# Column factors of the folded weights: on-chip transfers from ScalarE's queue in place of contraction-of-one products

## The chip, the core and the metric

The kernel runs on one core of one Trainium2 chip. The metric is the device time of the whole program in microseconds (us). The core has five engines that matter here: TensorE (PE in the profile) multiplies, with its weight loads listed apart as PEld; VectorE (DVE) and ScalarE (ACT) do elementwise work and empty the PSUM banks; GpSimd (POOL) does elementwise work in on-chip memory; SyncE (SP) issues nearly all transfers. ScalarE can issue transfers too. Whoever issues them, they are carried out by 16 DMA engines.

## The reference, cut to what matters

```python
X = np.fft.fft(np.fft.fft(x, axis=1), axis=2).real     # x: (8, 3008, 256) float32
h = X.reshape(24064, 256) @ w_in                       # w_in: (256, 2048)
g = h * (1.0 / (1.0 + np.exp(-1.702 * h)))             # quick gelu
out = g @ w_out                                        # w_out: (2048, 256)
```

A Fourier mixing over positions and channels is followed by a two-layer block with a quick gelu. Both weight matrices reach the kernel as 64-bit values, viewed as pairs of 32-bit words; the kernel makes float32 values of them on the chip.

## The kernel before, in words

**What is computed where.** The transform along the 256 channels is never done on the data. It is folded into the first weights: `fold_w(n)` (line 457) multiplies the tables `cd` with 512 columns of `w_in`, and `wcs[0]` and `wcs[1]` (each 128 x 2048) receive the cosine and the sine half. The transform along the 3008 positions is done on the data in two steps (`mix_first` or `mix1`, then `stage2`) and gives `pq`, blocks of 512 positions. Row 0 of the sine half is special: there the data row carries the alternating-sign component, which belongs neither to cosine nor to sine. `nyquist` (line 357) spreads that data row over all 128 partitions (`nb`), and its weights, row 0 of `wcs[1]`, are needed as a column, one value for each hidden unit on its own partition. These are the column factors: `af1` (128 x 16, column f for hidden units 128 f to 128 f + 127) and `af2`, twice that.

**How the columns are made.** `first_row(n)` (line 467) makes four columns. For each, a product with a contraction of one turns a 1 x 128 piece of row 0 into a 128 x 1 column of a PSUM bank (`psf`), with the constant `twos` as the other operand. Two ScalarE instructions then take the four columns out of the bank: a copy into `af2` (line 472) and a copy scaled by 0.5 into `af1` (line 473). There are four such groups, n = 0 to 3.

**The main loop.** `steps` numbers the work: 8 batches, 3 blocks of positions, 2 halves of a block and 8 pairs of hidden blocks (NP = 8). The first 8 steps (t = 0 to 7) take the weights while they are still being made. Step t runs `hidden(t)` (two banks `pa` and `pb`, 16 products; ScalarE copies `pa` to `v`), `rows(t)` on VectorE (which needs `v`, `nb` and two columns of `af2`, and ends with `reversed_sum`, line 539), `activate(t)` on ScalarE one step later, and `product(t - 3)`, which multiplies by `w_out`. From step 8 on, `middle(t)` writes `nb` times `af1` into a bank (line 566) before TensorE adds to it, and the second product is done with fewer multiplications (lines 596 to 671).

**Weights arriving.** `load_in(n)` and `load_out(n)` (lines 370 and 375) load a quarter of a weight matrix, 1 MB each. `clamp` (POOL), `squares`, `low_up` and `low_down` (ACT) and `high` (DVE) turn the 64-bit values into float32, and `finish_in` or `finish_out` (POOL) adds the parts. `load_in(2)` and `load_in(3)` feed `fold_w(2)` and `fold_w(3)`, which are placed in steps 3 and 5.

**What sets the order.** Each engine takes its instructions in program order, and the order is written out by hand: prologue, then the loop with the tables `extra`, `early` and `rows_at`. `early` says in which step `fold_w` runs, `rows_at` in which step `first_row` runs (before: n = 0 in the prologue, n = 1, 2, 3 in steps 1, 4 and 6). PSUM banks without a fixed tag are taken in turn from the list `spare`, so an allocation that is dropped moves all later ones. In step 5 the list is cut to four banks, and `hidden(5)` takes two others by name.

**Transfers.** SyncE issues in this order around the change: spill of the first batch's mixed rows to DRAM (`spill_first`, line 305), `fill` (line 328) which brings them back transposed in two parts, `load_out(0)`, `load_in(2)`, eight more spill pieces, `load_out(1)`, the second `fill`, `load_in(3)`, `load_out(2)`, `load_out(3)`, `load_matrices`, and then the input of the second batch (`turn` and `load_x`, lines 185 to 196). All transfers, from either queue, take eight completion semaphores in turn. The issue of a transfer first waits until the transfer before it on the same semaphore, eight places earlier, has landed, and a queue does not pass a waiting instruction.

Of the kernel before, what the change touches and what calls it, by code (L numbers as in the profile page):

```python
# [27 lines left out]
F32 = mybir.dt.float32  # L28
U32 = mybir.dt.uint32
ALU = mybir.AluOpType  # L30
ACTF = mybir.ActivationFunctionType
# [15 lines left out]
def view(ap, offset, *dims):  # L47
    return bass.AP(ap.tensor, ap.offset + offset, [list(d) for d in dims])


def free(ap, offset, *dims):
    return bass.AP(ap.tensor, ap.offset + offset, [list(ap.ap[0])] + [list(d) for d in dims])
# [59 lines left out]
def kernel(ctx: ExitStack, tc, x, w_in, w_out, tab1, tab2, out):  # L112
    nc = tc.nc
# [7 lines left out]
    const = ctx.enter_context(tc.tile_pool(name="const", bufs=1, space=SB))  # L121
# [17 lines left out]
    wcs = [const.tile([128, DF], F32, tag=f"wcs{i}", name=f"wcs{i}") for i in range(2)]  # L139
# [2 lines left out]
    wo, wt = wot[:, 0], wot[:, 1]  # L142
    af1, af2 = (const.tile([128, NF], F32, tag=f"af{i}", name=f"af{i}") for i in (1, 2))
    ones = const.tile([1, 128], F32, tag="ones", name="ones")
    twos = const.tile([1, 1], F32, tag="twos", name="twos")

    psu = ExitStack()
    o_banks = [psp.tile([128, 512], F32, tag=f"o{i}", name=f"o{i}") for i in range(2)]
# [6 lines left out]
    def ring(tag):  # L155
        at, size, count = rings[tag]
        i = turns[tag] = turns.get(tag, -1) + 1
        return big[:, at + i % count * size:at + (i % count + 1) * size]
# [7 lines left out]
    def bank(name, tag=None):  # L166
        if tag is None:
            tag = spare.pop(0)
            spare.append(tag)
        if tag in ("o0", "o1"):  # L170
            return o_banks[int(tag[1])]
        return (rest if tag[0] == "o" else psp).tile([128, 512], F32, tag=tag, name=name)
# [140 lines left out]
    def warm(n):  # L313

        ps = bank("warm")
        for _ in range(n):
            nc.tensor.matmul(ps[:], lhsT=wcs[0][:, 0:128], rhs=wcs[0][:, 0:512], start=True, stop=True)
# [65 lines left out]
    def prepare(key):  # L383


        pre[key] = ring("s"), ring("m"), ring("r").bitcast(U32)
# [70 lines left out]
    def fold_w(n):  # L457
        ps = [bank("psw") for _ in range(2)]
        for i in range(2):
            for cs in range(2):  # L460
                nc.tensor.matmul(ps[cs][:], lhsT=cd[:, i, cs, :], rhs=wst[n][:, i, :], start=(i == 0), stop=(i == 1))
        for cs in range(2):

            nc.scalar.copy(wcs[cs][:, n * 512:(n + 1) * 512].rearrange("p (f c) -> p f c", f=4),
                           free(ps[cs][:], 0, [1, 4], [4, 128]))

    def first_row(n):

        ps = bank("psf")
        for f in range(4 * n, 4 * n + 4):  # L470
            nc.tensor.matmul(ps[:, f:f + 1], lhsT=wcs[1][0:1, f * 128:f * 128 + 128], rhs=twos[:], start=True, stop=True)
        nc.scalar.copy(af2[:, 4 * n:4 * n + 4], ps[:, 4 * n:4 * n + 4])
        nc.scalar.activation(af1[:, 4 * n:4 * n + 4], ps[:, 4 * n:4 * n + 4], ACTF.Copy, scale=0.5)


    NP = NF // 2
# [8 lines left out]
    def width(t):  # L485

        return 226 if steps[t][1:3] == (0, 1) else 256

    def two(ap, n):
        return free(ap, 0, [256, 2], [1, n])  # L490
# [42 lines left out]
    def reversed_sum(out, by, x, y, n, op):  # L533

        full, rest = divmod(n, RUN)
        for at, blocks, m in ((0, full, RUN), (full * RUN, 1, rest)):
            if m:
                ins = [free(z[:], at, [256, 2], [RUN, blocks], [1, m]) for z in (x, y)]
                nc.vector.tensor_tensor(free(out, at + m - 1, [by, 2], [RUN, blocks], [-1, m]), *ins, op=op)  # L539

    def rows(t):
        b, blk, hh, p = steps[t]
        n = width(t)
        nb, ks = nbt[b, blk], slice(hh * 256, hh * 256 + n)
        v, pa, pb = vb.pop(t)
        h = ht[t] = ring("h").rearrange("p (a f n) -> p a f n", a=2, f=2)
        dif = sp.tile([128, 512], F32, tag="v", name="dif")
        nc.vector.tensor_tensor(two(h[:], n), two(v[:], n), two(pb[:], n), op=ALU.add)
        for i in range(2):
            f = 2 * p + i  # L550
            nc.vector.scalar_tensor_tensor(dif[:, i * 256:i * 256 + n], nb[:, ks], af2[:, f:f + 1],
                                           pb[:, i * 256:i * 256 + n], op0=ALU.mult, op1=ALU.subtract)
        reversed_sum(h[:, 1, 0], 256, pa, dif, n, ALU.add)

    def activate(t):
        g = free(ht[t][:], 0, [256, 4], [1, width(t)])
        nc.scalar.activation(g, g, ACTF.Gelu_apprx_sigmoid)
# [11 lines left out]
    def begin(t, cs=0):  # L569

        n = width(t)
        for i in range(2):
            halves(xb[t][:, i * 256:i * 256 + n], *operands(t, cs, i), start=False, stop=(cs == 1))
# [13 lines left out]
    def activate_back(t):  # L587
        nc.scalar.activation(back(t), back(t), ACTF.Gelu_apprx_sigmoid)  # L588
# [239 lines left out]
    for e in odds:  # L828
# [1 line left out]
    nc.vector.memset(flat[:, 6144:6176], 0.0)  # L830
    nc.vector.memset(free(pair[:, 0, 0], 0, [2 * NJ * NM, 2], [16 * 2 * NM, 2], [1, 2 * NM]), 0.0)
    nc.vector.memset(ones[:], 1.0)
    nc.vector.memset(twos[:], 2.0)
    ends = n0 + 4 - 28 * NM
    nc.sync.dma_start(out=free(w0, 0, [28 * NM, 2], [1, ends]),
                      in_=view(tab1, 0, [tab1.shape[1], 128], [28 * NM, 2], [1, ends]))
# [47 lines left out]
    warm(1)  # L884
    fold_w(0)
    warm(1)
    first_row(0)
    prepare(out0)
    finish_in(1)
    clamp(out0)  # L890
# [19 lines left out]
    n = len(steps)  # L910
# [4 lines left out]
            at(t - 1, bounds, key)  # L915
        at(t + 1, finish, key)
    early[3], early[5] = 2, 3
    rows_at = {1: 1, 4: 2, 6: 3}
    for t, c in ((0, 2), (1, 3)):
        at(t, load_out, c, nc.sync)  # L920
    at(3, load_matrices)
# [29 lines left out]
    for t in range(n + LAG):  # L951
        if t < NP:
            if t == NP - 3:
                spare[:] = [tag for tag in spare if tag[0] == "o"] + ["b2"]
            hidden(t)
            if t == NP - 1:
                middle(NP)
                begin(NP)
                nc.gpsimd.memset(wcs[1][0:1, :], 0.0)
            if t == 0:  # L960
                low_up(in2)
                nyquist(0, 0)
                low_down(in2)
            if t in rows_at:
                first_row(rows_at[t])
            if t >= LAG:
                product(t - LAG, 0, None)
            if t in early:
                fold_w(early[t])
            if t:  # L970
                activate(t - 1)
            rows(t)
            if t == NP - 1:
                doubled(NP)
                middle(NP + 1)
        else:
            after, special = (any(fn in (mix1, stage2) for fn, _ in extra.get(k, ())) for k in (t - 1, t))
            if t < n:
                begin(t, 1)
            if t == NP:  # L980
                activate(t - 1)
            if t < n:
                forward(t)
            if after and t + 1 < n:
                middle(t + 1)
            opening = (t - LAG) % NP == 0 and t >= NP + LAG
            one, other = (t - LAG, (1, 2, 4, 7)), (t - LAG - 1, (5, 6, 3))
            if opening:
                small_products(*other)
            cut = 0 if opening and not after else 3 if after else 2  # L990
            product(t - LAG, 0, cut)
            if after:
                small_products(one[0], one[1][:1])
                small_products(other[0], () if opening else other[1][:1])
            if t + 1 < n:
                begin(t + 1)
            if not opening:
                small_products(other[0], other[1][after:])
            product(t - LAG, cut, 6 if t - LAG == last else None)
            small_products(one[0], one[1][after:])  # L1000
            swap(t - LAG - 2)
            if t < n:
                backward(t)
            if t + 1 < n:
                doubled(t + 1)
            if t < n:
                activate_back(t)
                sums(t, nc.gpsimd)
            if t + 2 < n and not special:
                middle(t + 2)  # L1010
            combine_small(t - LAG - 1)
            if t - LAG == last:
                product(last, 6, None)
            sums(t - 1, nc.vector)
            deeper(t - 2, 0)
            deeper(t - 3, 1)
        if t == NP:
            psu.close()
            low = ctx.enter_context(tc.tile_pool(name="low", bufs=1, space=PS))
            pot["low"] = low.tile([128, 3 * 512], F32, tag="low", name="low")  # L1020
        if t >= LAG:
            combine(t - LAG)
            combine_last(t - LAG - 2)
            turn_last(t - LAG - 3, 0)
            turn_last(t - LAG - 4, 1)
        if t >= NP:
            spare[:] = [f"b{t % 2}"] * special + ["b2"]
        for fn, args in extra.get(t, ()):
            fn(*args)
# [28 lines left out]
```

## Time and profile before

The time before is 1876.94 us, the median of 3 runs (1874.98 to 1878.47). The profiled execution has a span of 1875.6 us.

| engine | busy us | share of the span | instructions |
|---|---|---|---|
| PE | 1853.0 | 99% | 23600 |
| PEld | 1414.9 | 75% | 23600 |
| DVE | 1532.0 | 82% | 2245 |
| ACT | 1148.9 | 61% | 2248 |
| POOL | 962.4 | 51% | 1058 |

The share is an average over the whole span. The columns are made in its first 80 us, where other things can set the pace. The table by stage shows the difference; each number is busy time in the stretch, and DMA is the mean busy share of the 16 DMA engines.

| stretch, us | PE | DVE | ACT | POOL | DMA share | what runs |
|---|---|---|---|---|---|---|
| 26 to 40 | 12.28 | 9.09 | 9.96 | 8.09 | 0.81 | folds 0 and 1, columns 0 |
| 40 to 49 | 9.00 | 7.33 | 7.42 | 3.64 | 0.91 | steps 0 to 2, columns 1 |
| 49 to 57 | 7.31 | 7.48 | 6.45 | 4.41 | 1.02 | step 3, fold 2 |
| 57 to 64 | 6.75 | 6.79 | 5.87 | 3.69 | 0.94 | step 4, columns 2 |
| 64 to 73 | 9.00 | 5.87 | 1.81 | 4.68 | 0.76 | step 5, fold 3 |
| 73 to 80 | 7.00 | 1.70 | 6.19 | 1.06 | 1.04 | step 6, columns 3 |
| 400 to 1000 | 598.89 | 498.51 | 373.24 | 302.59 | 0.36 | main loop |

In the main loop TensorE is busy nearly all the time, so a delay in the first 80 us that moves the start of the loop moves the end. The line of a group in the profile names the engine, the tile written and the tile read; the text after `[idle before <-` says what ended the idle time ahead of it. The wait of a transfer's issue is listed under SPq.

### The profile page before, as it was taken

The numbers are of one execution on the slowest core, as the hardware profiler recorded it, in microseconds if no ns is written. First come the engines' busy times: TensorE is split into PE (matmuls) and PEld (weight loads), VectorE is DVE, ScalarE is ACT, GpSimd is POOL, SyncE is SP. The second block draws the span as 40 slices with busy tenths as digits, with TensorE's granted clock in tenths as the row PEclk, the third lists the DMA queues.
The fourth block names the chain that finished last, engine by engine and source line by source line (L and its number), as shares of the span: only waits on it lengthen the run. The fifth ranks groups of instructions, "written<-read, shape, count | busy, mean of one in ns | idle before, by whom it ended". The sixth has DMA issues, their size and how long they took to land.

```text
span 1875.6 us, 55597 instructions
## 1 busy us (share of the span) xinstructions
PE 1853.0 (99%) x23600; PEld 1414.9 (75%) x23600; DVE 1532.0 (82%) x2245; ACT 1148.9 (61%) x2248; POOL 962.4 (51%) x1058
## 2 busy tenths in 40 slices
PE   8999999999999999999999999999999999999998
PEld 5567778777777777777777777777778777778776
DVE  7788878888789877988788877898788888878874
ACT  6655655666666666666565666656666656656663
POOL 4577335744467443673347733485435754444442
PEclk9999999999999999999999999999999999999999
DMA  8732351336221362305513165042631231212211
GB/s 275 180 51 17 80 88 20 51 51 115 27 17 47 52 123 19 52 17 94 80 16 52 23 115 56 13 63 44 111 26 24 19 51 47 28 16 18 20 22 23
DMA packets 145415, 105.21 MB, mean 56 GB/s; under 512 B 104914, under 2 KB 127986, under 8 KB 143984
## 3 DMA queue, kind: packets, MB, share of 16 engines
q1 hardware_dynamic: 143952, 101.14, 32.7%
q8 instruction: 186, 3.05, 0.7%
q10 hardware_dynamic: 1216, 0.52, 0.1%
q14 instruction: 61, 0.50, 0.1%
HBM read 58.38 MB, written 48.01 MB: 57 GB/s over the span
## 4 chain that ended last, share of the span: by engine, by line
PE 89%; DVE 5%; ACT 3%; DMA 2%; issue 1%; POOL 0%; SPq 0%; DVEq 0%; ACTq 0%; POOLq 0%
PE x L495 33%; PE o L495 25%; PE low L659 23%; PE o L659 4%; DMA big<-in_moe_w_in_dram 2%; DVE big L625 2%; PE ps L246 1%; PE ps L348 1%; DVE big L762 1%; DVE big L539 1%; ACT x L566 1%; ACT xt L249 0%; DVE big L671 0%; ACT big L581 0%; PE po L495 0%
## 5 line engine op out<-in xcount | busy, mean ns | idle before, releaser
L596 POOL TENSOR_TENSOR big<-big 128x256 f32<-128x256 f32 (+1 forms) x376 | 348.7, 927 | 848.9 <-ACT big L588 731.3
L495 PE MATMUL x<-pq,wcs 128*64 128x256 f32 (+1 forms) x6016 | 778.0, 378 | 5.7 <-ACT x L566 3.1
L625 DVE TENSOR_TENSOR big<-big 128x512 f32<-128x512 f32 (+1 forms) x736 | 640.0, 884 | 30.9 <-PE low L659 14.5
L495 PE MATMUL o<-big,wo 128*64 128x256 f32 (+1 forms) x4800 | 628.4, 376 | 0.4 <-DVE big L603 0.3
L495 PEld LDWEIGHTS x<-pq,wcs 128*64 128x64 f32 x6016 | 416.4, 137 | 194.1 <-issue 14.6
L495 PEld LDWEIGHTS o<-big,wo 128*64 128x64 f32 x4800 | 346.2, 137 | 147.7 <-DVE big L603 1.2
L578 ACT ACTIVATE g<-x 128x512 f32<-128x512 f32 (+1 forms) x376 | 221.7, 590 | 376.1 <-PE x L495 375.0
L539 DVE TENSOR_TENSOR big<-g,x 128x512 f32<-128x512 f32 (+2 forms) x440 | 254.2, 589 | 204.3 <-ACT big L581 203.6
L659 PE MATMUL low<-big 128*64 128x128 f32 (+1 forms) x5888 | 385.0, 270 | 1.9 <-issue 1.9
L659 PEld LDWEIGHTS low<-big 128*64 128x64 f32 x5888 | 340.2, 137 | 30.1 <-issue 2.1
L566 ACT ACTIVATE x<-nb,af 128x256 f32<-128x256 f32 (+1 forms) x752 | 352.7, 469 | 12.2
L597 POOL TENSOR_TENSOR big<-big 128x256 f32<-128x256 f32 (+1 forms) x376 | 358.9, 954 | 0.0
L581 ACT ACTIVATE big<-x 128x512 f32<-128x512 f32 (+1 forms) x376 | 220.4, 586 | 202.5 <-PE x L495 180.3
L588 ACT ACTIVATE big<-big 128x512 f32<-128x512 f32 (+1 forms) x376 | 231.8, 616 | 44.4 <-DVE big L539 43.1
L659 PE MATMUL low<-big,wo 128*64 128x128 f32 (+1 forms) x2944 | 223.3, 271 | 0.1
L659 PEld LDWEIGHTS low<-big,wo 128*64 128x64 f32 x2944 | 175.0, 137 | 3.6 <-DVE big L625 0.4
L604 DVE TENSOR_TENSOR big<-big 128x512 f32<-128x512 f32 (+1 forms) x188 | 149.9, 798 | 6.5
L603 DVE TENSOR_TENSOR big<-big 128x512 f32<-128x512 f32 (+1 forms) x188 | 137.1, 729 | 4.6 <-POOL big L596 4.6
L659 PEld LDWEIGHTS o<-big,wo 128*64 128x64 f32 x1472 | 94.4, 138 | 24.9 <-issue 0.3
L659 PE MATMUL o<-big,wo 128*64 128x128 f32 (+1 forms) x1472 | 112.4, 272 | 0.1
L762 DVE TENSOR_TENSOR big<-big,low 128x512 f32<-128x512 f32 (+3 forms) x184 | 109.1, 610 | 3.5
L218 POOL TENSOR_TENSOR xt<-xt 111x510 f32<-111x510 f32 x56 | 78.2, 1397 | 4.4
(103 smaller groups left out, 973.2 us busy)
## 6 DMA issues: line engine op xcount, KB each, us to landing
out_dram<-os SPq DMA_DIRECT2D x284, 64.0 KB
Td<-xt SPq DMA_DIRECT2D x14, 768.0 KB
t<-Td SPq DMA_DIRECT2D x7, 1536.0 KB
xt<-in_x_dram SPq DMA_DIRECT2D x14, 512.0 KB
xt<-Xr SPq DMA_DIRECT2D x14, 512.0 KB
nb<-pq SPq DMA_DIRECT2D x23, 256.0 KB
out_dram<-os SPq DMA_DIRECT2D x96, 56.0 KB
Xr<-in_x_dram SPq DMA_DIRECT2D x7, 752.0 KB
```

Source lines behind the costliest of these rows:

```text
L495: nc.tensor.matmul(out[c0:c0 + 64], lhsT=lhs[:, c0:c0 + 64], rhs=rhs, skip_group_check=True, **how)
L539: nc.vector.tensor_tensor(free(out, at + m - 1, [by, 2], [RUN, blocks], [-1, m]), *ins, op=op)
L566: nc.scalar.activation(x[:, i * 256:i * 256 + n], nbt[b, blk][:, hh * 256:hh * 256 + n], ACTF.Copy, scale=af1[:, f:f + 1])
L578: nc.scalar.activation(two(g[:], n), two(xb[t][:], n), ACTF.Copy, scale=2.0)
L581: nc.scalar.activation(front(t), two(xb[t][:], width(t)), ACTF.Gelu_apprx_sigmoid)
L588: nc.scalar.activation(back(t), back(t), ACTF.Gelu_apprx_sigmoid)
L596: eng.tensor_tensor(right(t, S1, n), left(t, A21, n), right(t, A22, n), op=ALU.add)
L597: eng.tensor_tensor(left(t, S3, n), left(t, A11, n), left(t, A21, n), op=ALU.subtract)
L603: eng.tensor_tensor(s2, s1, a11, op=ALU.subtract)
L604: eng.tensor_tensor(s4, a12, s2, op=ALU.subtract)
L625: nc.vector.tensor_tensor(out, i0, i1, op=how)
L659: nc.tensor.matmul(o, lhsT=lhs, rhs=rhs, start=first_in, stop=(p == NP - 2), skip_group_check=True)
```

## The change

The columns are no longer made by products. After `fold_w(n)` has copied 512 columns into `wcs[1]`, ScalarE's queue issues four transfers, each from 128 values in a row of partition 0 to one column of `af1` on 128 partitions, 4 bytes a piece. `first_row(n)` becomes one ScalarE instruction that doubles four columns of `af1` into `af2`. Its place moves: in the loop it now stands after `activate(t - 1)` and ahead of `rows(t)`, and n = 0 moves from the prologue to step 0. The 16 products, four PSUM banks, the constant `twos` and four ScalarE copies go. The purpose is to free TensorE and the banks from work that only moves values.

```diff
+        for f in range(4 * n, 4 * n + 4):
+            nc.scalar.dma_start(out=af1[:, f:f + 1], in_=free(wcs[1][0:1, f * 128:(f + 1) * 128], 0, [1, 128], [1, 1]))
 
     def first_row(n):
 
-        ps = bank("psf")
-        for f in range(4 * n, 4 * n + 4):
-            nc.tensor.matmul(ps[:, f:f + 1], lhsT=wcs[1][0:1, f * 128:f * 128 + 128], rhs=twos[:], start=True, stop=True)
-        nc.scalar.copy(af2[:, 4 * n:4 * n + 4], ps[:, 4 * n:4 * n + 4])
-        nc.scalar.activation(af1[:, 4 * n:4 * n + 4], ps[:, 4 * n:4 * n + 4], ACTF.Copy, scale=0.5)
+        nc.scalar.activation(af2[:, 4 * n:4 * n + 4], af1[:, 4 * n:4 * n + 4], ACTF.Copy, scale=2.0)
...
     fold_w(0)
     warm(1)
-    first_row(0)
     prepare(out0)
...
-    rows_at = {1: 1, 4: 2, 6: 3}
+    rows_at = {0: 0, 1: 1, 4: 2, 6: 3}
...
-            if t in rows_at:
-                first_row(rows_at[t])
             if t >= LAG:
                 product(t - LAG, 0, None)
             if t in early:
                 fold_w(early[t])
             if t:
                 activate(t - 1)
+            if t in rows_at:
+                first_row(rows_at[t])
             rows(t)
```

The added loop stands at the end of `fold_w`. The dropped lines for `twos` (its allocation and its memset) are left out of the diff.

## The prediction

> **What bounds the kernel now.** The page's list of engines puts TensorE at 99% of the span, so I read first the chain that ended last, to see whether this holds in the first 80 us, where the edit is. It does not. The chain in order of time (start us, length us, what) from 28 us on:
>
> ```profile
> 28.95 8.80 DMA big<-in_moe_w_in_dram
> ...
> 37.77 3.75 DMA Td<-e
> ...
> 41.59 0.38 SPq L328
> ...
> 42.06 10.86 DMA big<-in_moe_w_in_dram
> ...
> 52.95 1.16 ACT big L391
> ...
> 57.25 1.08 PE pa L495 x8
> 58.34 0.86 PE pb L495 x8
> 59.20 0.98 PE psf L471 x8
> ```
>
> The reader is to see that until 52.95 the end is set by transfers in SyncE's queue, one handing over to the next: `load_in(2)` lands, the last spill piece may go, when it has landed the second `fill` may go, behind it `load_in(3)`, and that landing starts the ScalarE work that leads to `fold_w(2)`'s weights and `hidden(4)` at 57.25. From there the chain is TensorE nearly without a gap. Next, SyncE's waits between 25 and 60 us (who waited for what: us in total, times, longest):
>
> ```profile
> SPq L305 <- DMA big<-in_moe_w_in_dram: 3.0, 1, 3.0
> ```
>
> The spill piece reads `e`, which was ready at 25.5; it waits for a weight load only because both use one completion semaphore. So the semaphore a transfer gets can put it on the path. Last, the timeline of ScalarE and of SyncE's issues around 40 us (start, length, instruction, idle before):
>
> ```profile
> 25.51 0.36 ACTq L305 DMA_DIRECT2D Td<-e  x1
> 38.19 0.36 SPq L378 DMA_DIRECT2D big<-in_moe_w_out_dram  x1
> 39.80 0.58 ACT L464 COPY wcs<-psw 128x512 f32<-128x512 f32 x1 [0.27 <-PE psw L461]
> 59.13 1.05 PE L471 MATMUL psf<-twos,wcs 1*128 1x1 f32 x8
> ```
>
> The weights row of `fold_w(1)` is complete at 39.80 + 0.58 = 40.38, later than the last spill (37.77) and `load_out(1)` (38.19) are issued.
>
> **What the Trainium skill says.** "Perfetto Trace Analysis", section "DMA Instruction — HWDGE (DVE, Sync)": the profiled window of a transfer is the issue alone; the move and the completion write come after it. The trace agrees: 0.36 us is shown for the spill at 25.51, but the fill that needs it starts at 27.92. "DMA: Bandwidth & Descriptors", section "Queues, rings and completion order": SP and ACT each own a row of rings on the same 16 DMA engines, so ScalarE's transfers do not pass for free; here the engines are 0.91 busy from 40 to 49 us. "TensorE: Matmul & The Clock Gate", section "What's actually happening": an idle window of about 3.4 us halves the clock. The trace shows a case: after TensorE's 2.20 us idle before 109.32 the granted clock is 0.50 to 0.56 from 109.5 to 113.
>
> **The change part by part.**
>
> *Products removed.* Four groups of about 1.05 us of TensorE (4.2 us). The first (32.06) and second (44.50) lie while the chain is in transfers: nothing. Those at 59.20 and 74.94 are on the chain, 0.98 us each: at most -2.0 us.
>
> *Hand-over of semaphores.* I read the queues of the built changed kernel. The four transfers after `fold_w(1)` come, in the turn of eight, one turn ahead of the last spill (which now waits for the first of them), `load_out(1)` (for the second), the second `fill` (the third) and `load_out(2)` (the fourth). SyncE does not pass a waiting issue. So the first transfer's landing replaces that of `load_in(2)` as what releases the last spill.
> - Issue: from 40.4, when the copy ends. One issue costs 0.36 (row above) to 0.55 us (the median of the 128-partition `nb` transfer); I take 0.42, so they start at 40.4, 40.8, 41.2 and 41.7.
> - Landing, counted from the issue: no row shows a 4-byte transfer. The spill above took 27.92 - 25.51 = 2.4 us with 64 KB to DRAM. Packets on SyncE's queue cost 32.7% of 16 x 1875.6 us over 143,952, or 68 ns each; 128 pieces over 16 engines are 8 x 68 ns = 0.55 us. The skill's DMA page puts a fixed 2.0 us (a fit for GpSimd's path, section "Anatomy of one DMA — SWDGE (gpsimd) path"). I take 2.0 + 0.6 = 2.6; ends 1.9 and 4.
> - Last spill: 40.4 + 2.6 = 43.0 instead of 37.77. `load_out(1)`: the later of 40.8 + 2.6 and 43.0 + 0.45, so 43.5 instead of 38.19, +5.3. `fill`: the spill's 2.4 us on, 45.4 instead of 41.59, +3.8. `load_in(3)`: 45.9 instead of 42.06, +3.8.
> - Landing of `load_in(3)`: by its issue +3.8; by the data ahead of it, which starts with `load_out(1)` after the engines have run empty, +5.3 less about 0.3 for the dip that lay between `load_out(1)` and `fill` (the engines are 0.76 busy from 42 to 44 us). The data are ahead in the ring, so I take +5.0: 57.9 instead of 52.92. Ends 3.8 and 7 from the landing's ends.
>
> ScalarE is free by then: its wait for `load_out(1)` ends near 50, and `low_up`, `low_down`, the copy of `v` and one gelu follow by 55. `hidden(4)` starts at 62.3.
>
> *Order on ScalarE, step 4.* The four issues after `fold_w(2)` (1.7 us) stand ahead of two gelus and `v`, and `af2` now stands behind the gelu of step 3. Counted from `hidden(4)`, `af2` is there at 5.0 to 6.1 us, VectorE needs it at 5.73 as before, so `rows(4)` ends at about 7.3 to 7.5. Before, TensorE went on with `hidden(5)` at 64.03 - 57.25 = 6.78 without waiting for `rows(4)`; with the `psf` banks gone the turn of banks gives it the bank that `rows(4)` still reads. So the 0.98 us saved is lost in a wait: +0.7 net.
>
> *Order on ScalarE, steps 5 to 7.* After `fold_w(3)` ScalarE has no gap from 73.10 to 79.3, then 1.11 us idle. Four issues add 1.7; that idle falls away; the other 0.98 us of TensorE no longer counts, because `middle(8)` on ScalarE releases it: 1.7 - 1.1 - 0.1 = +0.5 net.
>
> *Clock.* TensorE's gap ahead of `hidden(4)` grows from 0.70 to some 3.7 us, and two gaps of 1.6 and 2 us appear. A halved window of 3.4 us costs up to 1.7 us; the first is mostly under the wait of step 4; a quarter of one: +0.4, an estimate.
>
> *At nothing.* The changed `first_row(0)` delays `rows(0)` by about 2 us, and with it the fold of `load_in(2)`: `psw` would run 55 to 58.7, under the wait to 62.3. The loads of the second batch are issued up to 16 us later (one waits for the transfers after `fold_w(3)`) but are first read on GpSimd at 110.40, some 12 us after they would land. Later semaphore turns are the same, as 16 transfers are two full turns.
>
> Sum: 5.0 + 0.7 + 0.5 + 0.4 = +6.6; 1876.94 + 6.6 = 1883.5 us.
>
> **The rivals.**
> - *Only the products count.* The columns land early enough to hold nobody. For it: they are 512 bytes each. Against it: their issue cannot come before 40.38, and the spill they hold left at 37.77. Then -2.0: 1874.9, no slower.
> - *Only ScalarE's issue time counts*: `load_in(3)` has slack or catches up, because the engines serve a shorter queue. For it: the engines dip to 0.76 from 42 to 44. Against: the chain goes through that landing. Then +0.7 + 0.5: 1878.1.
> - *The turned columns are slow.* For it: the `nb` transfer, which also reads one partition, moved 79 packets between 96 and 102 us, 76 ns each one after another with all engines shown busy; 128 pieces in such a row would be 9.7 us. Against: those packets have 2 KB, so the port's rate, 27 GB/s, explains them. At 25 ns a piece a landing takes 5 us and four in a row queue up: about 8 us for the landing, +10.5 on the load and some 2.5 behind it; 1876.94 + 13 = 1890.
>
> **How the numbers follow.** Forecast 0.72, only products 0.08, only issue time 0.08, slow columns 0.12. The forecast's own ends are 3.8 + 0.7 + 0.3 = +4.8 (1881.7) and 7 + 1.1 + 0.9 + 1.7 = +10.7 (1887.6). The range reaches down to the second rival and up to the third: 1878 to 1890; about 0.16 is left outside. Faster by over 0.2% means below 1873.2, which no case gives by itself: 0.05. Within 0.2% (to 1880.7) lie two rivals less that share, and a little of the forecast: 0.15. Slower: 0.80.
>
> **What would show it.** Right: the last spill issued near 43 and waiting for a transfer into `af`; `load_in(3)` landing near 58; TensorE idle 3 to 4 us ahead of `hidden(4)`; a wait of TensorE on VectorE's `rows(4)` ahead of `hidden(5)`; issues of 0.36 to 0.55 us. Wrong: `load_in(3)` landing within 1 us of 52.9, or an `af2` instruction waiting many us for its columns.

## The result, and the profile after

The changed kernel takes 1891.65 us (median of six runs, 1884.83 to 1896.26) against 1877.56 us (1874.98 to 1878.47) on the same chip: ratio 1.0078, 95% interval 1.0057 to 1.0099. It is slower, as predicted, but by 14.1 us where 6.6 were predicted, and it lies 1.65 us above the top of the range.

The chain that ended last in the kernel after, in order of time (start us, length us, what); its lines are one to three lower than those of before, so L466 is the transfer and L470 the doubling in `first_row`:

```profile
41.38 0.50 ACTq L466
...
43.90 0.59 ACT v L507
...
45.93 1.06 ACT big L405
...
46.99 0.10 ACT af L470
...
47.12 0.88 DVE dif L548 x2
...
50.82 2.12 DVE big L422
...
55.16 2.37 POOL wst L436
...
57.57 5.41 PE psw L460 x8
...
65.44 2.06 DMA af<-wcs
...
81.89 3.46 DMA af<-wcs
...
92.50 1.77 PE x L492 x8
```

The reader is to see that SyncE's row of transfers, which carried the chain of before up to 52.95, is gone from it. In its place stand the four issues on ScalarE, then `v(0)` behind them, then the doubling `af2` behind `low_down`, then VectorE's `rows` and `high`, GpSimd's sum and `psw` of `fold_w(2)`. The two pieces `DMA af<-wcs` are landings of columns, but ScalarE itself issues or computes all through both, and e11 and e16 below show that nobody loses by them. TensorE, in the timeline of its instructions (start, length, instruction, idle before and what ended it), waits in four places in this stretch; the line at 62.90, `hidden(4)`, has no wait:

```profile
48.86 1.08 PE L492 MATMUL pb<-pq,wcs 128*64 128x256 f32 x8 [2.46 <-DVE big L536]
...
57.57 5.40 PE L460 MATMUL psw<-wst,small 128*128 128x512 f32 x8 [2.44 <-POOL wst L436]
62.90 1.08 PE L492 MATMUL pa<-pq,wcs 128*64 128x256 f32 x8
...
70.51 1.08 PE L492 MATMUL pa<-pq,wcs 128*64 128x256 f32 x8 [1.90 <-DVE t L334]
...
92.50 1.77 PE L492 MATMUL x<-pq,wcs 128*64 128x226 f32 x8 [4.21 <-ACT x L563]
```

Three of these four are followed by products that take longer than their kind: `psw` 5.40 us in place of 3.70, for one. The clock record has three stretches of 3.4 us at half clock there, from 58.1, 71.8 and 92.3 us; before had its first at 109.6. The length of these stretches agrees with the window of about 3.4 us of which the Trainium skill speaks in "TensorE: Matmul & The Clock Gate", "What's actually happening". The waits ahead of them do not: the skill has the clock halved after an idle window of that length, and here 2.44 and 1.90 us of idle were enough, while 2.46 us ahead of 48.86, 2.54 us in e1 and 2.58 us in e13 were followed by full speed. So the length of a wait alone does not decide it in these traces.

ScalarE's timeline and the summary of its sixteen issues (shortest, median and longest in ns, first and last start) show the price of an issue, and the waits of SyncE (who for what: us in total, times, longest) show the hand-over of semaphores that the prediction had built on:

```profile
41.38 2.48 ACTq L466 DMA_DIRECT2D af<-wcs  x4
43.90 0.59 ACT L507 COPY v<-pa 128x512 f32<-128x512 f32 x1 [2.55 <-PE psn L364]
...
56.79 1.15 ACT L390 ACTIVATE big<-big 128x1024 f32<-128x1024 f32 x1 [1.39 <-DMA big<-in_moe_w_in_dram]
...
62.14 0.59 ACT L463 COPY wcs<-psw 128x512 f32<-128x512 f32 x1 [1.61 <-PE psw L460]
...
81.89 3.45 ACTq L466 DMA_DIRECT2D af<-wcs  x4
```

```profile
L466 ACTq DMA_DIRECT2D af<-wcs x16: 477/618/1632, 32.7 to 84.7; - x16
```

```profile
SPq L304 <- DMA af<-wcs: 7.6, 3, 5.0
...
SPq L377 <- DMA af<-wcs: 1.7, 1, 1.7
```

A group of four issues takes 2.51, 2.48, 2.44 and 3.45 us of ScalarE. Fifteen of the issues take 0.48 to 0.63 us; one in the last group takes 1.63. The other six kernels below that issue the sixteen transfers from ScalarE also have one of 1.1 to 1.6 us in the last group; what it waits for, the profile does not show. Three spill pieces wait 7.6 us together for transfers into `af`, one of them 5.0, and `load_out(1)` 1.7 more; the first reader of `load_in(3)` starts at 56.79 in place of 52.95. But the copy of `wcs` at 62.14 does not wait for the work behind that load, it waits for `psw`, and TensorE goes from `psw` to `hidden(4)` at 62.90 without idle time. So the late load holds nobody there. Where the distance to the kernel before builds up, from the starts of these products in the two traces:

| first product of | before, us | after, us | later by |
|---|---|---|---|
| `hidden(0)` | 39.70 | 40.66 | 1.0 |
| `psw`, `fold_w(2)` | 52.85 | 57.57 | 4.7 |
| `hidden(4)` | 57.25 | 62.90 | 5.7 |
| `hidden(5)` | 64.03 | 70.51 | 6.5 |
| `psw`, `fold_w(3)` | 69.36 | 77.53 | 8.2 |
| step 8 (`x`) | 81.91 | 92.50 | 10.6 |
| step 9 (`x`) | 86.18 | 98.31 | 12.1 |

The rest comes in the main loop, and there the distance does not stay the same. Counted at the starts of the `nb` transfers it is 12.1 us at 94 us of the kernel before, 10.2 at 329, 15.8 at 480, 13.0 at 1085 and 14.2 at 1756. One of the jumps is in TensorE's timeline of the changed kernel: it stands idle for 3.52 us ahead of 422.42, with no wait that the profile shows. So the loop itself moves the distance between these two traces by 2 to 4 us.

### The profile page after: what moved, and what is told of

It reads as the page before. It is cut to its first block, busy times and chain, and to the rows that moved or that the text cites. A ratio compares the mean times of both kernels' runs of the same rounds, so it can differ in the third digit from the quotient of the medians.

```text
span 1889.7 us, 55550 instructions
## 1 busy us (share of the span) xinstructions
PE 1853.0 (98%) x23568; PEld 1420.7 (75%) x23568; DVE 1532.3 (81%) x2244; ACT 1149.8 (61%) x2244; POOL 962.5 (51%) x1058
## 4 chain that ended last, share of the span: by engine, by line
PE 89%; DVE 5%; ACT 3%; DMA 2%; issue 1%; POOL 0%; ACTq 0%; SPq 0%; DVEq 0%; POOLq 0%
PE x L492 33%; PE o L492 25%; PE low L656 23%; PE o L656 4%; PE ps L347 1%; PE ps L245 1%; DVE big L622 1%; PE psw L460 1%; ACT x L563 1%; DVE big L759 1%; DVE big L536 1%; DMA big<-in_moe_w_in_dram 1%; ACT xt L248 1%; DMA wo<-in_tab_dram 0%; ACT big L578 0%
```

## The experiments

Times are medians; "over before" is the difference to the median of the kernel before on the same chip (1876.2 to 1877.0 us), and the interval is that of the ratio. A and B are the two theories at the start: A, ScalarE spends its own time in order on the issues and what stands behind them comes late; B, the prediction's, the semaphores handed to SyncE make its loads late. C, D and L came up on the way.

**What the columns are worth if they cost nothing (e1).** The four `nc.scalar.dma_start` of `fold_w` are taken out, and the columns with them: `af1` and `af2` hold constants.

```
+    nc.vector.memset(af1[:], 1.0)
+    nc.vector.memset(af2[:], 2.0)
-        for f in range(4 * n, 4 * n + 4):
-            nc.scalar.dma_start(out=af1[:, f:f + 1], in_=...)
     def first_row(n):
-        nc.scalar.activation(af2[...], af1[...], ACTF.Copy, scale=2.0)
+        pass
```

> The changed kernel with the sixteen transfers taken out; af1 and af2 are filled once with 1 and 2, and first_row does nothing. Left out of the computation: the column factors themselves. This is the benefit of the change alone, without its price. Theory A (the time of ScalarE in order is the price) and theory B (the hand-over of completion semaphores to SyncE is the price) both say 1874 to 1878 us, load_in(3) landing near 53, psw of fold_w(2) starting near 53 and middle(8) near 82. Above 1884 us both fall: then taking the products away, and the turn of the PSUM banks that goes with it, would itself be what costs.

Measured: 1880.83 us, 3.8 over before, ratio 1.0019 (1.0012 to 1.0026). It falls between the two limits that were set, but nobody had expected a loss: with no transfer left, taking the products away alone makes the kernel slower.

**ScalarE's time without transfers (e2).** As e1, `first_row` kept, and in the place of the issues:

```
+        for _ in range(4):
+            nc.scalar.copy(wst[n][:, 0, :], small[:, 0:512])
```

> As the kernel with free columns, but in the place of the four issues ScalarE makes four copies of 128x512 to a dead tile, of about 0.6 us each; first_row stays where the change put it. Left out: the column factors. No transfer, so no semaphore is handed over and nothing waits for a landing. Theory A (ScalarE's time): 1884 to 1891 us, load_in(3) lands near 53 yet psw(2) starts at 56 to 58 and TensorE stands idle ahead of it. Theory B (hand-over): 1874 to 1879 us.

Measured: 1884.66 us, 7.7 over before, 1.0045 (1.0033 to 1.0058), and `psw` at 57.6, 15.8 us after `hidden(0)` (13.1 in e1 and before). As A said, at the lower end, though half of the loss was already in e1.

**The transfers on SyncE (e3).** `nc.scalar.dma_start` becomes `nc.sync.dma_start`.

> The changed kernel with the same sixteen transfers issued by SyncE's queue. ScalarE has none of the 10 us of issues; SyncE waits for wcs in its own order, so its loads are at least as late as after the change. Theory A (ScalarE's time): 1876 to 1882 us, though load_in(3) lands at 56 or later. Theory B (late loads of SyncE): 1886 us or more, with psw(2) at 57 or later.

Measured: 1896.37 us, 19.4 over before, 1.0109 (1.0095 to 1.0122). A's number is missed by far, and B's (1886 or more, `psw` at 57 or later) is met: `psw` starts at 60.64. But the cause is not B's. ScalarE's timeline of this kernel:

```profile
100.28 0.20 ACT L470 ACTIVATE af<-af 128x4 f32<-128x4 f32 x1 [10.79 <-DMA af<-wcs]
```

On SyncE's queue the last columns stand behind loads, and ScalarE stands 10.8 us ahead of the last doubling, as it stood 3.7 us ahead of the first. The run says nothing on A against B.

**The half-clock stretches (e4).** Ten unused products in the gaps, so that TensorE has something to run:

```
+        if n == 2:
+            warm(3, ps[0])          # ahead of psw of fold_w(2)
...
+            if t == NP - 3:
+                warm(2, bank("warm", "b2"))
             hidden(t)
+            if t == NP - 1:
+                warm(5, bank("warm", "b1"))
```

> The changed kernel with ten products added that are used by nothing, in TensorE's three gaps: three ahead of psw of fold_w(2), two ahead of hidden(5), five ahead of middle(8)'s begin. The waits stay as they are. If the stretches at half the TensorE clock (58 to 62, 72 to 75 and 92 to 96 us in the changed kernel) come from the gaps and each costs 1.5 to 1.8 us: 1885 to 1888 us and at least two of the three stretches gone. If the stretches come by themselves or cost nothing: 1890 to 1894 us.

Measured: 1890.10 us, 13.1 over before, 1.0077 (1.0064 to 1.0089). All three stretches are gone (granted clock 0.996 to 1.000 over the runs, 0.993 to 0.997 in the changed kernel), and the time hardly moves. In the profiles this kernel is 2.8 us quicker from `hidden(0)` to step 9, and gives back 1.7 us of that by the first of the `low` products (at 125 us). So the stretches go when the gaps are filled, and removing them in this way is not worth their length.

**The addresses (e5, e6, e7).** All profiles of the changed kernel and of e1 to e4 started later than before (`hidden(0)` at 40.7 to 43.7 us, not 39.7), and taking `twos` away had moved `xt`, `big` and what lies behind them 32 bytes down. That was theory C. e5 and e7 put a tile back into the place; e6 takes it from the kernel before (shortened):

```
e5, e7: +    pad = const.tile([1, 1], F32, tag="pad", name="pad")
e6:     -    twos = const.tile([1, 1], F32, tag="twos", name="twos")
        -    ... rhs=twos[:] ...   copy to af2, scale=0.5 to af1
        +    ... rhs=ones[:, 0:1] ...   scale=2.0 to af2, copy to af1
```

> The changed kernel with a tile of the size of twos kept in its place and used by nothing. Taking twos away moved xt, big and all tiles behind it 32 bytes down in SBUF; this moves them back. Theory C (the addresses cost): in the profiles of the changed kernel and of e1 to e4 the load of w_in was issued at 9.3 to 11.3 us against 8.6 before and hidden(0) began at 40.7 to 43.7 us against 39.7; with the pad hidden(0) is back near 39.7 and the time falls by 1 to 4 us, to 1887.5 to 1890.5. Rival (the late start comes from run to run): 1890 to 1893 us, hidden(0) anywhere from 39.7 to 43.

> The kernel before without twos: its products of contraction one take a column of ones in its stead, af2 takes the factor of 2 on ScalarE and af1 none. As many instructions on each engine as before, the same values, but the tiles behind twos lie 32 bytes lower, as in the changed kernel. Theory C: 1878.5 to 1881 us and hidden(0) later than 40.5. Rival: 1876 to 1878 us.

> e1 (columns for nothing; their making is left out) with the pad. Theory C: 1875 to 1878 us, hidden(0) near 39.7, so that the benefit of the products taken away is 0 to 2 us and all of e1's 3.6 us over before were addresses. Rival: as e1, 1880 to 1882 us, and the products taken away bring a loss by some other way, the banks' turn or the place of first_row.

Measured: e5 1889.12 us, 12.8 over before, 1.0063 (1.0050 to 1.0075); e6 1875.79, 0.6 under, 0.9995 (0.9987 to 1.0003); e7 1881.83, 5.5 over, 1.0027 (1.0017 to 1.0038). C falls: e6 has the lower addresses and no loss, and e7 has the old ones, an early start (`hidden(0)` at 39.5) and e1's loss. e5's number lies in the range that C had given, but its `hidden(0)` is at 41.1, not back near 39.7, and its 12.8 us are not told apart from the changed kernel's 14.1. The start differs from run to run, and a delay there need not reach the end: e6's profile has `hidden(0)` 2.5 us later than before and its end 0.4 us later. It is the slowest of thirteen runs of e6, so it does not show that a late start costs nothing.

**The turn of the banks (e9, e10).** The products took a PSUM bank from the list `spare` four times. Without them every later tile gets another bank. e9 is e1, e10 the changed kernel, each with one step of the list in those four places:

```
     warm(1)
+    spare.append(spare.pop(0))
     prepare(out0)
...
+            if t in (1, 4, 6):
+                spare.append(spare.pop(0))
             if t >= LAG:
```

> e1 (columns for nothing; their making is left out), with the list of spare PSUM banks moved on by one at the four places where the kernel before took a bank for the products. No instruction more than e1, every later tile in the bank that it had before. Theory D (the banks' turn is what makes e1 and e7 slower than before by 3.6 to 5.5 us): 1874 to 1878 us, and hidden(5) no longer waits for the copy of psr. Rival E (the same loss by something else that went with the products): 1880 to 1882 us.

> The changed kernel with the banks' turn of before restored in the same way, nothing else. Theory D with losses that add up: 1885 to 1888 us. If the turn's loss lies beside that of ScalarE's issues, or theory D is wrong: 1889 to 1893 us.

Measured: e9 1875.14 us, 1.0 under before, 0.9995 (0.9987 to 1.0004); e10 1886.16, 10.0 over, 1.0050 (1.0038 to 1.0063). D holds: one step in a list of names, and e1's loss is gone. TensorE's timeline of e7, where the turn is not restored:

```profile
64.79 1.65 PE L491 MATMUL pa<-pq,wcs 128*64 128x256 f32 x8 [2.56 <-DVE t L335]
66.17 1.98 PE L491 MATMUL pb<-pq,wcs 128*64 128x256 f32 x8
```

and of e9, where it is:

```profile
62.52 1.08 PE L490 MATMUL pa<-pq,wcs 128*64 128x256 f32 x8
```

`hidden(5)` is given the banks b0 and b1 by name. In the turn of before, `psw` of `fold_w(2)` had used them last, and ScalarE had long copied that out. In the new turn it is `hidden(4)`, whose sums VectorE still reads in `rows(4)`: 2.56 us of waiting, and half clock after it. (The trace names the copy into `t`, which VectorE runs right behind `rows(4)`.)

**One transfer for a group (e8, e12).** The row is copied on one partition in the order in which the columns want it, so that 128 pieces of 16 bytes make the whole group, and `first_row` is put ahead of the gelu, for the first group ahead of `fold_w(1)` (that line is not shown); e8 has the pad, e12 the banks' turn:

```
-        for f in range(4 * n, 4 * n + 4):
-            nc.scalar.dma_start(out=af1[:, f:f + 1], ...)
+        nc.scalar.copy(wst[n][0:1, 0, :], ps[1][0:1, :])
+        nc.scalar.dma_start(out=af1[:, 4 * n:4 * n + 4], in_=free(wst[n][0:1, 0, :], 0, [4, 128], [1, 4]))
...
+            if t in rows_at:
+                first_row(rows_at[t])
             if t:
                 activate(t - 1)
-            if t in rows_at:
-                first_row(rows_at[t])
```

> The changed kernel with the pad, one transfer for a group instead of four (a copy of the sum's row on one partition, then 128 pieces of 16 bytes), and first_row put ahead of the gelu, for the first group ahead of fold_w(1). ScalarE's price for a group falls from 2.5 us to about 1.2 and the doubling stands behind nothing. Theory A (ScalarE's time and order is the price): 1878 to 1883 us, middle(8) by 86 and psw(2) by 55. Theory B (hand-over of semaphores, which stays): above 1886 us.

> The changed kernel with one transfer of 16-byte pieces for a group, first_row ahead of the gelu and for the first group ahead of fold_w(1), as in e8 but without its pad, and the banks' turn of before restored. The whole computation. Theory D: 1878 to 1882 us against 1884.0 of e8, so near before but not below it, as the products taken away are worth 2 us at most. Rival E: 1883 to 1886 us.

Measured: e8 1884.01 us, 7.7 over before, 1.0036 (1.0024 to 1.0048); e12 1882.02, 5.8 over, 1.0030 (1.0020 to 1.0041). e8 falls between the two theories, e12 at the upper edge of D's range. ScalarE in e12 ahead of step 7:

```profile
74.21 0.57 ACT L465 COPY wst<-psw 1x512 f32<-1x512 f32 x1
74.81 0.48 ACTq L466 DMA_DIRECT2D af<-wst  x1
...
82.01 0.20 ACT L470 ACTIVATE af<-af 128x4 f32<-128x4 f32 x1 [1.93 <-DMA af<-wst]
```

A group costs 1.1 us in place of 2.5, and here the landing, some 7 us after the issue, holds ScalarE.

**Landings, late loads and ScalarE's time apart (e11, e13 to e16).** e11 and e16 send the transfers into an unread tile (`out=af1` becomes `out=dump`, `af1` filled with ones), e16 with the banks' turn of before. e13 is the kernel before with four transfers of SyncE held back; e14 is e2 with the turn of before; e15 is e14 with the transfers held back as in e13 (shortened: the lines that keep each load's place in its ring are left out):

```
e13, e15:
-    load_out(1, nc.sync); fill(0, 4, NG)       # ahead of the loop
-    load_in(3, nc.sync)
             hidden(t)
+            if t == 1:
+                nc.scalar.copy(raw["out", 1][:, 0:1, 0].bitcast(F32), ones1[:])
+                load_out(1, nc.sync)
+                fill(0, 4, NG)
+                load_in(3, nc.sync)
+                load_out(2, nc.sync)
```

> The changed kernel with all sixteen transfers issued by ScalarE as there, but into a tile that nobody reads; af1 is filled with ones and doubled in the same place (left out: the column factors). ScalarE's issues and the semaphores handed to SyncE stay, nobody computes on what lands. Theory L (the rest between e2, 1884.7 us, and the changed kernel, 1889 to 1892 us, is the wait of af2 and of middle(8) for the landing, 1.9 to 3.5 us after the issue): 1883 to 1886.5 us. Theory B (that rest is the hand-over of semaphores, late loads): 1888 to 1892 us, with load_in(3) landing near 57.

> The kernel before with load_out(1), fill(0, 4), load_in(3) and load_out(2) sent by SyncE only after ScalarE's copy v(1), by one small copy of 128x1 on ScalarE ahead of them that writes where load_out(1) lands: load_out(1) goes out at 45, load_in(3) at 46 in place of 42.1, and lands at 56 to 57, as in the changed kernel. The whole computation. The prediction's step (late load_in(3) holds psw(2) and with it hidden(4)): 1880 to 1883 us and psw(2) at 57. Theory A (it waits beside other work, VectorE's chain of rows and high sets psw(2)): 1875.5 to 1878.5 us with psw(2) at 52.5 to 54.

> e9 (columns for nothing, left out of the computation; the banks' turn of before) with e2's four copies of 128x512 on ScalarE for each group. ScalarE's time alone against 1875.1 us of e9. Theory A: 1879 to 1883 us. If ScalarE's time costs only together with the other banks' turn: 1875 to 1877.5 us.

> e14 with the four loads of e13 sent late in the same way. If ScalarE's time and late loads together make what is left of the change (e10, 1886.2 us): 1884.5 to 1888 us. If late loads cost nothing also beside ScalarE's time: as e14, 1879 to 1883 us.

> e11 (all transfers issued by ScalarE into a tile that nobody reads; the column factors left out) with the banks' turn of before. Against e10 it lacks only the waits for the landing; against e14 it has real issues in place of copies, and the hand-over of semaphores. If landings cost nothing: 1885 to 1887.5 us, as e10. If they cost 2 us or more: 1880 to 1884 us.

| kernel | us | over before | ratio, 95% interval |
|---|---|---|---|
| e11 | 1889.61 | 13.4 | 1.0072 (1.0058 to 1.0085) |
| e13 | 1880.22 | 3.3 | 1.0018 (1.0008 to 1.0028) |
| e14 | 1883.94 | 7.0 | 1.0035 (1.0023 to 1.0048) |
| e15 | 1886.78 | 9.9 | 1.0051 (1.0039 to 1.0064) |
| e16 | 1886.75 | 9.8 | 1.0051 (1.0039 to 1.0064) |

L falls: e11 is as slow as the changed kernel and e16 as slow as e10, so nobody loses by waiting for what lands. A late load can cost time: e13 delays the transfers alone and is slower. Its chain is the prediction's chain, later:

```profile
44.93 9.70 DMA big<-in_moe_w_in_dram
...
54.66 1.16 ACT big L399
...
57.84 0.57 ACT v L518
58.41 0.50 ACT wcs L472
```

Counted from `hidden(0)` (38.70 here, 39.70 before), the load lands 2.7 us later than before, and `hidden(4)` starts 2.7 us later (20.25 us after `hidden(0)`, not 17.55), after 2.58 us of idle. The forecast had `psw` at 57; it starts at 52.67, so it is not what waits for the load. This profile is of the fastest of nine runs, 2.6 us under their median: its loop starts 2.1 us late (at the `nb` transfer near 94 us) and its end is 0.2 us late. So this trace shows the wait, and only the median shows a loss. The same edit on top of ScalarE's time, e15, has in TensorE's timeline

```profile
62.00 1.08 PE L500 MATMUL pa<-pq,wcs 128*64 128x256 f32 x8 [1.93 <-ACT wcs L471]
```

a wait for the `wcs` copy, which e14 does not have. Whether the changed kernel loses anything in this way is another matter. Its TensorE does not wait there, and neither does that of e4, e5, e10, e11, e16 or e17, which have the transfers. In e10:

```profile
61.15 3.70 PE L460 MATMUL psw<-wst,small 128*128 128x512 f32 x8
64.78 1.08 PE L492 MATMUL pa<-pq,wcs 128*64 128x256 f32 x8
```

In these kernels the first reader of the load starts 14.9 to 16.1 us after `hidden(0)`, in e15 18.2. So e15 comes out as slow as e10 with a load that is later than any of theirs. B as the cause of the changed kernel's loss is not shown. And A holds: e14 against e9 has four copies on ScalarE for each group and `first_row` where the change put it, nothing else, and the two intervals are far apart. e14's chain:

```profile
39.68 0.53 ACT wst L466
...
42.15 0.49 ACT v L507
...
45.13 0.10 ACT af L470
...
46.17 0.70 DVE big L536
...
47.00 1.97 PE pa L492 x8
...
74.43 0.53 ACT wst L466
...
81.52 0.96 ACT big L554
82.47 0.10 ACT af L470
...
84.34 1.98 PE pb L492 x8
```

The copies stand in the chain at two groups, after `fold_w(1)` and after `fold_w(3)`. In the first, `v(0)` and `af2` come late, so `rows(0)` does, whose bank the first product of `hidden(2)` wants: it starts 5.5 us after that of `hidden(1)`, in e9 2.5. In the last, the second half of `hidden(7)` starts 5.4 us after the first, in e9 2.5. Between the first products of `hidden(4)` and `hidden(7)`, with the group after `fold_w(2)` in between, both take 19.84 us: there ScalarE's time costs nothing. (The profile of e14 is again that of its fastest run, 3.1 us under the median.)

**The place of the doubling, and the shortest form (e17, e18).** e17 is e10 with `first_row` ahead of the gelu, and for the first group ahead of `fold_w(1)`; e18 is e12 with the last group's `first_row` back behind the gelu.

> e10 (the changed kernel with the banks' turn of before) with first_row put ahead of the gelu, and for the first group ahead of fold_w(1); all sixteen transfers as in the change, the whole computation. If the place of first_row carries 1 us or so at two groups (the gelu of 1.0 us stands in e14's chain ahead of the doubling): 1883 to 1885.5 us. If a landing then holds ScalarE instead, or the place is worth nothing: 1885.5 to 1888 us.

> e12 (one transfer of 16-byte pieces for a group, first_row early, banks' turn of before; the whole computation) with first_row of the last group back behind the gelu, where e12 waited 1.93 us for the landing. Theory A: 1879.5 to 1882 us, 0 to 2 us under e12's 1882.0, and not below the kernel before, since the copy of the row and the issue still take 1.1 us of ScalarE at each group.

Measured: e17 1884.26 us, 8.0 over before, 1.0044 (1.0030 to 1.0058); e18 1882.88, 6.6 over, 1.0037 (1.0024 to 1.0049). The place is worth some 2 us (10.0 to 8.0) or nothing, as the intervals overlap. e18 lies just above its range and gains nothing on e12: with the doubling behind the gelu it still waited 1.80 us for the landing. No form of the change comes out quicker than the kernel before, and e9 says why: free of all costs the columns are worth 1.0 us, and its interval contains none at all.

## Why the prediction was wrong

The step that failed is the path. The forecast put 5.0 of its 6.6 us on a late `load_in(3)` for which `hidden(4)` would wait, with TensorE idle 3 to 4 us there as the sign. It put ScalarE's order at 1.2 us in steps 4 to 7 and, for the changed `first_row(0)`, at nothing, under that wait. In the trace `hidden(4)` does not wait at all. The idle time, 2.44 us, is ahead of `psw` of `fold_w(2)`, and `psw` is late through ScalarE's order. So the direction was right, but not by the way that was given for it.

The sizes, by the differences of medians, depend on the order in which the parts are added, so the table has two orders: first with the banks' turn of before, then with that of the change. The runs are some 2 us apart within one kernel, so each size is good to 1 or 2 us.

| part | predicted | turn of before first | turn of the change throughout |
|---|---|---|---|
| products taken away | -2.0 at most, used up in the 1.2 | -1.0 (e9) | +3.8 with the turn (e1) |
| ScalarE's time and order | 1.2 in two steps, of which the bank is a part | +8.0 (e14 - e9) | +3.8 (e2 - e1) |
| real transfers in place of copies | +5.0, late loads | +3.0 (e10 - e14) | +5.8 (e11 - e2) |
| waits for the landing | 0 | 0 (e10 against e16) | 0 (e5 and after against e11) |
| turn of the banks | in the 0.7 of step 4 | +3.4 (e5, e11 and after, mean 13.4, less e10) | in the first row |
| clock | +0.4 | inside the others | inside the others |
| sum | +6.6 | +13.4 | +13.4 |

Each sum comes out at the changed kernel (14.1, 12.8 with the pad) because its last member is a run of that kernel or one as slow; it is no test of the parts. What holds in both orders is that ScalarE's time and order cost 3.8 to 8.0 us where 1.2 was put, and that the turn matters. The third row is open. e13 prices late loads at 3.3 us where they are the last to come, but in the traces with real transfers they are not; the longer issue of the last group (0.7 us over the median in e10 and e11) can be a part of it, and for the rest no run shows a cause.

ScalarE's order was mis-sized above all in the sentence under *At nothing*, that the changed `first_row(0)` delays `rows(0)` by 2 us under a wait that is longer anyway. An issue takes 0.62 us (the median), not 0.42 (0.55 was the upper end), and one took 1.63. `v(0)` starts at 43.90 where before it was 40.83, `rows(0)` is nearly 4 us later (first `dif` at 47.12, before 43.35), and on it wait not only the fold of `load_in(2)` and `psw` of `fold_w(2)` (57.57, where the prediction had 55) but also TensorE's next bank. Steps 5 to 7 were put at +0.5, because ScalarE had 1.11 us of idle to give; e14 shows some 2.9 us at `hidden(7)` alone, since the issues now stand ahead of `v(6)`, and they and a gelu ahead of `af2`, and with them of `rows(6)`. The other item put at nothing held: the second batch's loads went out up to 19 us later (85.37 for 66.14), and GpSimd's first reading of them, at 122.53, did not wait.

The hand-over itself held. The last spill waits for a transfer into `af` and leaves at 43.58 (43.0 predicted), `load_in(3)` leaves at 46.74 (45.9) and lands at 56.79 (57.9). The first transfer of the second group, issued at 41.38, lets that spill go 2.2 us later, which agrees with the estimate of 2.6 us worked out with the Trainium skill's fixed 2.0 us ("DMA: Bandwidth & Descriptors", "Anatomy of one DMA — SWDGE (gpsimd) path"); the next one, issued at 41.92, holds `load_out(1)` until 45.69, 3.8 us, and the first of all, issued at 32.66 beside the big loads, holds a spill piece until 38.77, 6.1 us. So no one figure fits. The load is 3.8 us later in the trace, not 5.0, and `psw` comes later still.

Step 4 foresaw the bank: `hidden(5)` waits for `rows(4)`, 1.90 us in the trace. What was not seen is that one bank wait is one of several: `hidden(2)`'s second half waits 2.46 us for `rows(0)`. The turn's size depends on what else is late: 3.8 + 1.0 = 4.8 us between e1 and e9, 3.6 between e11 and e16, 0.7 between e2 and e14. Why it is small beside ScalarE's time without real transfers stays open.

The clock: three stretches at half speed came with the gaps, where a quarter of one had been allowed. The prediction's own case, 2.20 us of idle ahead of 109.32, was already shorter than the window that it cited. In e14 the stretches lie in the chain twice (`pa` and `pb` at 1.97 and 1.98 us). e4 shows that they are not a cost of their own that can be bought back with idle products.

A delay at the start of the loop does not move the end by its whole length: the traces of e6 and e13 are 2.2 and 2.1 us late at the `nb` transfer near 94 us, and 0.4 and 0.2 us at the end.

Of the rivals, *slow columns* came nearest by its number, 1890, and was wrong by its reason: a landing takes 2.2 to 6.1 us where the trace bounds it, but e16, which computes on nothing that lands, is as slow as e10. The 25 ns a piece of that rival stand in no trace. *Only ScalarE's issue time*, put at 1878, named the part that is best shown, and had 1.2 us of it.

## What to carry to other kernels

Issuing a transfer from an engine that computes takes that engine's time in its order: 2.5 us for four small ones. Cost it by following every instruction queued behind it to its readers, and do not set it against another wait before that wait is known to stay the longer one. When several delays meet, what each one costs depends on which of the others is there, so measure it in both settings. Before optimising what an operation costs, build the version in which it costs nothing: here it was worth 1 us, which no form of the replacement could undercut. And when a tile is taken out of a rotating list, read the new owner of every later bank, since the loss by the turn alone (0.7 to 4.8 us, by what else was late) could be larger than the gain.

## What had not been expected of the hardware

A transfer of 128 pieces of 4 bytes holds the issuing queue for 0.62 us on ScalarE and for 0.59 on SyncE (medians of sixteen, changed kernel and e3); one of 16-byte pieces for 0.48 (e12). In the last group one of the four takes 1.1 to 1.6 us in all seven kernels that issue them from ScalarE, for no reason that the profile shows. The landing is not a constant: what waits for it goes on 2.2, 3.8 and 6.1 us after the issue in the changed kernel, and some 7 us in e12's last group. A shift of the large tiles by 32 bytes made no difference (0.9995, e6). And the half clock came after 1.90 us of idle and stayed away after 2.58 (e13).
